# A 20-product first pass and one interleaved table for both passes in a conv and feed-forward kernel

## The chip, the cores and the metric

The kernel runs on one core of a Trainium2 chip. The metric is the time of one execution on the device in microseconds (us); lower is better. The engines are named as in the profile: PE (TensorE, with PEld for its weight loads), DVE (VectorE), ACT (ScalarE), POOL (GpSimd) and SP (SyncE, which issues DMAs).

## The reference

A depthwise causal convolution with 7 taps (weights by softmax, one set for each of 8 heads) over x of (8, 4096, 192), then a feed-forward layer with the quick GELU, all in float32:

```python
w = np.exp(weight - max); w = w / (sum(w) + 1e-9)              # (8 heads, 7 taps)
out = np.einsum('hk,bskhg->bshg', w, x_unf)                    # 7 taps back in time, group = 24
x = out.reshape(8 * 4096, 192)
h = x @ w_in                                                   # (32768, 192) @ (192, 2048)
g = h * (1.0 / (1.0 + np.exp(-1.702 * h)))
return g @ w_out                                               # (32768, 2048) @ (2048, 192)
```

## The kernel before

The tokens are cut into 32 stages ("big"), each of 2 blocks of 512 tokens. In each stage there is a first product (conv output times w_in, `hidden`) and a second one (GELU output times w_out, `second`). Both are written as fast matrix multiplication schemes: sums and differences of blocks of the operands are formed, fewer products than in the plain form are made on PE, and the results are joined. Stage 0 (`first_step`, `second_first`) is done in another way, as it also unpacks the weights and forms their sums (`sums_w_in`, `add_forms`).

**First product.** `hidden` is called twice in a stage, for the two halves v of the columns of w_in. Each pass makes the 21 products of `TERMS`: a pair (sum of w_in blocks, sum of conv blocks). `product1` (L633) issues a product as two matmuls on 64 rows each, side by side on PE, into two PSUM banks. ACT copies results out of PSUM (`copy2`, L670), DVE joins them (`sum2`, L674), and ACT applies the GELU (`gelu`, L655 from PSUM and L659 from SBUF) into the big tile `g`. There are four PSUM tiles of two banks: x, y, z and sums. The products, copies, joins and GELUs stand in the program in the order that the body of `hidden` writes out by hand. `fetch` issues the next pass's first product ahead of its pass.

**Second product.** `second` walks the list `PLAN`. "go" issues one step (three matmuls of 32 columns for the main part and one for a side part, L1007), "sum" and "acc" form sums of blocks of `g` ("acc" by an accumulating DMA on POOL, L983; "sum" on DVE, L391 and L393), "seed" and "join" move results, "turn" and "store" transpose and store. `spot(i)` names blocks of `g`, `room` and `osbs` that hold GELU outputs and their sums; a spot is free once the products that read it are done.

**Conv of the stage after next.** It is made tap by tap, 21 taps for the three channels 1, 0 and 2, in this order. `tap` (L521) is one ACT multiply into a home: tap 0 goes to the conv tile, the others to halves of spots (`TAP_SPOTS`). The taps of channels 1 and 0 are then added together by accumulating DMAs on POOL (L541) listed in `LATER`; (b, i, j) under (c, k) means that behind tap k of channel c, tap j of channel b is added into its tap i, and i = 0 is the conv tile. Taps 1 to 6 of channel 2 are added by POOL (L523). A "tap" in `PLAN` or a `taps_at` in `hidden` draws the next one (`next_tap`): 14 in `second`, 7 in the first pass of the next stage's `hidden`. POOL then forms the sums of the conv (`sums_c`, L391 and L393), and DMAs on SP cross their halves over to the other 64 partitions (`cross`, L561), held in three sets in `conv_t`.

All engines run their instructions in program order; the framework sets a wait before an instruction whose operand another engine or a DMA still writes or reads. SP also loads x (L99) and stores the output (L936).

Of the kernel before, what the change touches and what calls it, by code (L numbers as in the profile page):

```python
# [15 lines left out]
def kernel(  # L16
# [29 lines left out]
    nc = tc.nc  # L46
# [81 lines left out]
    k15, k19, k20, k18, k16 = (room[:, i, :].rearrange("p (h n) -> p h n", h=2) for i in range(5))  # L128
# [27 lines left out]
    NB = 13  # L156
    C11, C12, C21, C22, C31, C32, V2, V3, V4, V5, V6, V7, V8, V1 = range(NB + 1)
    conv_t = consts.tile([P, 3, NB, T], F32)
    SUMS_C = [
        (V1, C31, "-", C11),  # L160
        (V2, V1, "-", C32),
        (V3, C12, "+", V2),
        (V4, C22, "+", V2),
        (V5, C21, "-", V4),
        (V6, C11, "-", V5),
        (V7, C22, "-", C21),
        (V8, C32, "-", C22),
    ]

    def place(big, b):  # L170

        if b == V1:
            return V8 if big % 2 else C31
        return C31 if b == V8 and big % 2 else b

    def own(big):
        return conv_t[:, big % 2 * 2, :, :]
# [6 lines left out]
        (18, 0, "+", 3),  # L184
        (0, 0, "+", 2),
        (12, 10, "n", 11),
        (13, 12, "-", 2),
        (16, 3, "+", 5),
        (17, 2, "+", 5),
        (5, 2, "+", 11),  # L190
        (14, 3, "-", 12),
        (15, 4, "+", 13),
        (19, 6, "+", 8),
        (8, 8, "-", 11),
        (11, 9, "+", 11),
        (9, 9, "-", 3),
        (3, 3, "0", 3),
        (20, 19, "+", 10),
        (12, 1, "-", 13),
        (4, 4, "n", 16),  # L200
        (10, 7, "-", 10),
        (11, 11, "-", 19),
        (7, 7, "+", 19),
# [3 lines left out]
        (14, V2), (10, C21), (20, V5), (6, V3), (19, V6), (0, C11), (17, C32), (5, V8), (4, V7), (8, V1), (12, C22),  # L207
        (9, C12), (13, V4), (3, V3), (15, C22), (16, V6), (2, V1), (1, C21), (11, C11), (7, V7), (18, C12),
# [38 lines left out]
    assert PIECE == CW * D and 3 * PIECE <= NB * T and 3 * PIECE <= 2 * NJ * XW and 3 * PIECE <= FORMS * NG * HD  # L247
# [153 lines left out]
    def sums_w_in(i):  # L401
        add_up(lambda j: w_in_s[:, j, :], *SUMS_W[i])
# [66 lines left out]
    def transpose_x(big, c, n=None):  # L469
# [9 lines left out]
    first_taps = [row(0, k) for k in (6, 7, 10, 11, 14, 15)]  # L479
# [4 lines left out]
        0: [conv_t[:, i, b : b + 2, :] for i in (1, 2) for b in (V2, V4, V6)],  # L484
# [12 lines left out]
    def conv(big, c, k, ns=slice(0, 2), times=vec.tensor_scalar_mul):  # L497
# [50 lines left out]
    def sums_c(big, i):  # L548
        add_up(
            lambda j: own(big)[:, place(big, j), :],  # L550
            *SUMS_C[i],
            eng=vec if big == 1 else nc.gpsimd,
        )

    def cross(big, b0, b1):
        for o in range(2):
            out, src = conv_t[halves[1 - o], 1, b0:b1, :], own(big)[halves[o], b0:b1, :]
            if big == 1 and b1 - b0 > 1:
                act.copy(out, src)
            else:  # L560
                nc.sync.dma_start(out=out, in_=src)  # L561

    def copy_over(b):

        for o in range(2):
            act.copy(conv_t[halves[1 - o], 1, b, :], own(0)[halves[o], b, :])

    waiting = {True: [], False: []}  # L570
    given = {True: 0, False: -1}
    pieces = []

    def cross_now(early, big, b0, b1):
        if early or big == 1:
            cross(big, b0, b1)
        else:
            pieces.extend((big, b, min(b + 3, b1)) for b in range(b0, b1, 3))

    def cross_piece():  # L580
        if pieces:
            cross(*pieces.pop(0))

    def cross_when(early, *what):
        if given[early] < what[0] - 1:
            waiting[early].append(what)
        else:
            cross_now(early, *what)

    def give(early, big):  # L590
        given[early] = big
        for what in waiting[early]:
            cross_now(early, *what)
        waiting[early].clear()

    def prepare(big):

        v1 = place(big, V1)
# [5 lines left out]
        cost = 0.34 if big == 1 else 0.0  # L604
# [8 lines left out]
        yield "", cost, lambda: sums_c(big, 0)  # L613
        yield f"first {big}", 0.0, lambda: cross_when(True, big, v1, v1 + 1)
        yield "", 0.0, lambda: cross_when(False, big, 0, C31)
        for i in range(1, len(SUMS_C)):
            yield "", cost, lambda i=i: sums_c(big, i)
        rest = (C31, V8) if big % 2 else (C31 + 1, NB)
        yield f"all {big}", 0.0, lambda: cross_when(False, big, *rest)
# [8 lines left out]
    def product1(slot, a, b, big, v, first=False):  # L628
        pair = conv_t[:, big % 2 : big % 2 + 2, place(big, b), :]
        for h in range(2):  # L630

            src = pair[halves[h], :, :] if h == big % 2 else pair[halves[h], ::-1, :]
# [9 lines left out]
    def terms(big, v, slot, *ts, first=False):  # L642
        for t in ts:
            product1(slot, *TERMS[t], big, v, first)
            first = False
# [3 lines left out]
    def gelu(b, u, v, src):  # L649
# [3 lines left out]
        if isinstance(src, list):  # L653
            for h in range(2):
                act.activation(  # L655
                    dst[:, :, h, :], src[h].rearrange("p (o t) -> p o t", o=2), AF.Gelu_apprx_sigmoid
                )
        else:
            act.activation(  # L659
                dst.rearrange("p o h t -> p h o t"),  # L660
                src.rearrange("p h (o t) -> p h o t", o=2),
                AF.Gelu_apprx_sigmoid,
            )

    def bank(t, h):
        return t[h] if isinstance(t, list) else t[:, h, :]

    def copy2(dst, src):
        for h in range(2):
            act.copy(bank(dst, h), bank(src, h))  # L670

    def sum2(op, dst, a, b):
        for h in range(2):
            op(*(bank(t, h) for t in (dst, a, b)))  # L674
# [6 lines left out]
    def hidden(big, v, x, z, y, sums, work, fetch, last=lambda: None):  # L681

        def pe(slot, *ts, first=False):
            terms(big, v, slot, *ts, first=first)

        def taps_at(n):
            for _ in range(0 if v else n):
                next_tap()  # L690

        def early(i):
            for item in (EARLY_G if big > 1 else EARLY_G_1)[i] if v else ():
                sum_g(*item)


        if v:
            pe(z, 7, first=True)
            give(True, big)
        if v:  # L700
            pe(sums, 12)
            copy2(k15, sums)
            pe(x, 5, 17)
        else:
            pe(x, 5)
            pe(sums, 12)
            copy2(k15, sums)
            pe(x, 17)
            taps_at(1)
        gelu(B11, 0, v, x)  # L710
        if not v:
            pe(z, 7, first=True)
        pe(sums, 0)
        copy2(k16, sums)
        taps_at(2)
        last()
        def turn_next():
            if big + 2 < N_BIG:
                need(f"done {big + 1}")
                turn_x(big + 2)  # L720

        early(0)
        if not v:
            work(2.0 if big > 1 else 1.6, big + 1)
        elif big == 1:
            work(3.2)

        pe(y, 6, 14, first=True)
        sum2(vec.tensor_sub, x, z, k15)
        early(1)  # L730
        if not v or big == 1:
            work(1.6 if big > 1 else 1.2, big + 1)
        pe(sums, 13)
        copy2(k19, sums)
        pe(x, 2)
        copy2(k18, x)
        taps_at(2)
        pe(z, 11)
        pe(sums, 20, 10)
        sum2(vec.tensor_sub, k15, y, k19)  # L740
        gelu(B12, 0, v, sums)
        pe(x, 4)
        copy2(k20, x)
        sum2(vec.tensor_sub, k19, z, k19)
        early(2)
        if not v or big == 1:
            work(1.1, big + 1)
        gelu(B22, 1, v, k19)
        gelu(B22, 0, v, k15)
        taps_at(2)  # L750
        pe(y, 8)
        pe(sums, 1, 9, first=True)
        pe(y, 15)
        if v and big == 1:
            turn_next()
        elif not v:
# [557 lines left out]
```

## Time and profile before

| | |
|---|---|
| median of 3 runs | 2273.91 us (2273.06 to 2274.0) |
| the profiled execution | 2273.34 us, of it 2271.6 us span from the first to the last instruction |
| PE busy | 2263.5 us (100% of the span) |
| DVE, ACT, POOL busy | 1764.2, 1693.3, 984.9 us |
| moved by DMA | 329.87 MB, 145 GB/s in the mean |

In rows of the timeline and the groups, "L633 PE MATMUL slot<-conv_t,w_in_s" is line 633's matmul that writes a tile named slot; x4 is how many follow each other; "[2.43 <-ACT g L655]" is idle time before it and what ended it. The rows of windows give the length, then for PE, PEld, DVE, ACT and POOL the busy time (and instructions), the granted PE clock, the share of the DMA engines and GB/s. Rows of DMA issues give count, size of each and median time from issue to landing.

### The profile page before, as it was taken

To read this page: it belongs to the slowest core of one execution; us is meant where nothing else is said; L and a number is where in the kernel's file an instruction comes from. 1 tells how busy PE (TensorE), PEld (TensorE's weight loads), DVE (VectorE), ACT (ScalarE), POOL (GpSimd) and SP (SyncE) were. 2 spreads that over 40 slices of the span, in tenths; PEclk is the share of its full clock that TensorE was granted. 3 is DMA by queue.
4 is the path that set the end of the run, shared out by engine and by line. 5 is a ranking of instruction groups with operands and counts; after the bars stand their busy time and mean duration, and the time that the engine had idled before them with its cause. 6 is when DMAs were issued, how large, how long until landed. Compare 5 with 4: busy or idle time off the path is not lost.

```text
span 2271.6 us, 61499 instructions
## 1 busy us (share of the span) xinstructions
PE 2263.5 (100%) x25214; PEld 1210.6 (53%) x25214; DVE 1764.2 (78%) x2591; ACT 1693.3 (75%) x3175; POOL 984.9 (43%) x1008
## 2 busy tenths in 40 slices
PE   9999999999999999999999999999999999999999
PEld 4375555555555555555555555555555555555556
DVE  8987777887777877778877778777887777877777
ACT  8777787777877777777778777787777877777754
POOL 1544454344553445534445434454344553444500
PEclk9999999999999999999999999999999999999999
DMA  9987778777787777777777887778777787776643
GB/s 206 154 158 146 152 139 154 151 147 147 145 154 146 143 145 152 144 150 151 145 152 139 152 156 146 151 138 155 152 144 145 151 149 150 146 144 125 115 99 71
DMA packets 294970, 329.87 MB, mean 145 GB/s; under 512 B 120736, under 2 KB 208800, under 8 KB 294688
## 3 DMA queue, kind: packets, MB, share of 16 engines
q0 software_dynamic: 82704, 196.32, 48.9%
q1 hardware_dynamic: 210336, 129.22, 25.8%
q8 instruction: 198, 3.24, 0.6%
q14 instruction: 84, 0.69, 0.1%
q10 hardware_dynamic: 1648, 0.39, 0.1%
HBM read 53.15 MB, written 25.17 MB: 34 GB/s over the span
## 4 chain that ended last, share of the span: by engine, by line
PE 98%; DMA 1%; DVE 0%; ACT 0%; issue 0%; POOL 0%; SPq 0%; DVEq 0%; ACTq 0%; POOLq 0%
PE slot L633 35%; PE slot L1007 33%; PE sums L633 16%; PE sums L1007 12%; PE slot L839 2%; DMA g<-g 0%; DMA xin<-in_x_dram 0%; ACT conv_t L1114 0%; DVE xt L473 0%; DVE conv_t L504 0%; SPq L99 0%; ACT conv_t L357 0%; POOL g L983 0%; ACT conv_t L356 0%; POOL g L541 0%
## 5 line engine op out<-in xcount | busy, mean ns | idle before, releaser
L633 PE MATMUL slot<-conv_t,w_in_s 64*128 64x512 f32 x3740 | 861.2, 591 | 0.3 <-DVE w_in_s L376 0.3
L1007 PE MATMUL slot<-g,w_form 128*32 128x256 f32 x7024 | 711.1, 379 | 0.1
L633 PEld LDWEIGHTS slot<-conv_t,w_in_s 64*128 64x128 f32 x3740 | 375.6, 187 | 425.6 <-issue 358.9
L393 DVE TENSOR_TENSOR g<-g 128x1024 f32<-128x1024 f32 x372 | 451.5, 1242 | 3.2
L1007 PEld LDWEIGHTS slot<-g,w_form 128*32 128x32 f32 x7024 | 375.6, 110 | 118.1 <-DMA g<-g 0.8
L541 POOL DMA_DIRECT2D g<-g x232 | 225.3, 1084 | 476.0 <-DVE room L393 174.8
L633 PE MATMUL sums<-conv_t,w_in_s 64*128 64x512 f32 x1660 | 407.7, 589 | 0.3 <-DVE w_in_s L376 0.3
L659 ACT ACTIVATE g<-room 128x1024 f32<-128x1024 f32 x310 | 326.0, 1078 | 65.9 <-DVE room L674 40.5
L521 ACT ACTIVATE g<-xt,cw 128x512 f32<-128x512 f32 x534 | 367.8, 725 | 3.7
L1007 PE MATMUL sums<-g,w_form 128*32 128x256 f32 x2648 | 368.8, 379 | 0.0
L1032 ACT COPY room<-slot 32x256 f32<-32x256 f32 x434 | 158.5, 365 | 226.0 <-PE slot L1007 223.1
L1007 PE MATMUL slot<-g,w_out_s 128*32 128x256 f32 x4080 | 318.8, 380 | 0.0
L983 POOL DMA_DIRECT2D g<-g x124 | 126.3, 1019 | 375.9 <-PE slot L1007 143.1
L523 POOL TENSOR_TENSOR conv_t<-conv_t,g 128x512 f32<-128x512 f32 x180 | 250.1, 1389 | 49.0 <-ACT g L521 41.8
L633 PEld LDWEIGHTS sums<-conv_t,w_in_s 64*128 64x128 f32 x1660 | 171.6, 187 | 186.4 <-issue 150.0
L670 ACT COPY room<-slot 128x512 f32<-128x512 f32 x434 | 231.6, 602 | 38.8 <-PE slot L633 38.5
L1007 PEld LDWEIGHTS slot<-g,w_out_s 128*32 128x32 f32 x4080 | 164.7, 110 | 129.0 <-ACT g L655 22.7
L655 ACT ACTIVATE g<-slot 128x512 f32<-128x512 f32 x334 | 180.6, 598 | 46.5 <-POOL conv_t L393 19.0
L393 POOL TENSOR_TENSOR conv_t<-conv_t 128x256 f32<-128x256 f32 x180 | 195.5, 1099 | 11.8 <-DMA conv_t<-g 3.1
L1007 PEld LDWEIGHTS sums<-g,w_form 128*32 128x32 f32 x2648 | 177.8, 110 | 37.6
L674 DVE TENSOR_TENSOR room<-slot,room 128x512 f32<-128x512 f32 x248 | 156.2, 681 | 35.5 <-ACT room L670 35.5
L541 POOL DMA_DIRECT2D conv_t<-g x116 | 145.5, 1254 | 86.3 <-DVE room L391 36.7
(207 smaller groups left out, 2793.9 us busy)
## 6 DMA issues: line engine op xcount, KB each, us to landing
g<-g POOLq DMA_DIRECT2D x124, 512.0 KB, 5.9
g<-g POOLq DMA_DIRECT2D x236, 256.0 KB, 4.8
xin<-in_x_dram SPq DMA_DIRECT2D x240, 180.0 KB, 4.2
conv_t<-conv_t SPq DMA_DIRECT2D x180, 192.0 KB, 3.2
conv_t<-g POOLq DMA_DIRECT2D x118, 256.0 KB, 6.5
out_dram<-osbs SPq DMA_DIRECT2D x186, 128.0 KB, 5.2
g<-room POOLq DMA_DIRECT2D x31, 512.0 KB, 5.4
g<-osbs POOLq DMA_DIRECT2D x30, 512.0 KB, 4.7
```

What stands on the lines that cost most here:

```text
L393: eng.tensor_sub(v(dst), v(a), v(b))
L521: act.mul(home, conv_src(big, c, k), cw[:, c, k : k + 1])
L523: nc.gpsimd.tensor_add(dst, dst, home)
L541: nc.gpsimd.dma_start(out=out, in_=src, accum_op=ALU.add)
L633: nc.tensor.matmul(slot[h], w_in_s[halves[h], a, v * P : (v + 1) * P], src, start=first, stop=True, skip_group_check=True,)
L655: act.activation(dst[:, :, h, :], src[h].rearrange("p (o t) -> p o t", o=2), AF.Gelu_apprx_sigmoid)
L659: act.activation(dst.rearrange("p o h t -> p h o t"), src.rearrange("p h (o t) -> p h o t", o=2), AF.Gelu_apprx_sigmoid,)
L670: act.copy(bank(dst, h), bank(src, h))
L674: op(*(bank(t, h) for t in (dst, a, b)))
L983: nc.gpsimd.dma_start(out=spot(dst), in_=spot(a), accum_op=ALU.add)
L1007: nc.tensor.matmul(dst, w, t, start=first, stop=last, skip_group_check=True)
L1032: act.copy(to, d)
```

## The change

- The first pass of a stage uses a scheme of 20 products, the second its 21. Each pass has its own sums of w_in (`SUMS_W`, 25 and 21 operations on 128 columns each, for 20 on 256 columns before).
- Both passes are one list, `HIDDEN`: products ("mm", pass, term, PSUM tile, first), copies on ACT ("a") or DVE ("v"), joins, GELUs and the rest, interleaved. Copies go to nine places `KS` in `room` and in spots 19, 20, 0 and 1. GELUs can negate their input.
- The sums of the conv are held once, with one copy across, in the places that `places_of` gives; four of them (`SUMS_L`) lie in halves of spots 14 and 17 (`SPOT_V`). POOL forms most of them in "piece" items of `PLAN`, and SP crosses them there.
- `TAP_SPOTS` has spot 20 for 17, channel 2's homes are other halves of spots, some of which are homes of other taps too. 17 taps are drawn in `second`, 4 in `hidden`.

```diff
-    KEPT_LATE, TAP_SPOTS = 3, {0: (13, 15, 17), 1: (11, 10, 16), 2: (14, 16, 18), 3: (15, 16, 19)}
+    KEPT_LATE, TAP_SPOTS = 3, {0: (13, 15, 20), 1: (11, 10, 16)}
+    TAP_HALVES = {2: ((11, 2), (18, 0), (18, 2), (13, 0), (18, 0), (18, 2)), 3: ((12, 2), ...)}
...
+    KS = [room[:, 1, :], room[:, 3, :], room[:, 2, :], room[:, 0, :], room[:, 4, :],
+        spot(19)..., spot(20)..., spot(0)..., spot(1)...]
+    SPOT_V = {16: (14, 2), 17: (14, 0), 18: (17, 2), 19: (17, 0)}
+    SUMS_F = [(12, 1, "+", 4), (12, 12, "-", 5)]
+    SUMS_L = [(16, 0, "-", 6), (17, 7, "-", 3), (18, 0, "-", 2), (19, 0, "-", 1)]
...
-    def hidden(big, v, x, z, y, sums, work, fetch, last=lambda: None):
...
+    HIDDEN = [
+        ("mm", 0, 8, 1, 1), ("tap",), ("tap",), ("mm", 0, 0, 2, 1), ("copy", "a", "k0", "p1", 1), ("mm", 0, 2, 3, 1),
+        ("copy", "v", "k5", "p0", 1), ("copy", "a", "k3", "p2", 1), ("mm", 0, 16, 1, 0),
+        ("copy", "a", "k6", "p3", 1), ("mm", 1, 13, 0, 0), ("copy", "v", "k4", "p1", 1), ("mm", 0, 3, 2, 0),
...
+    ]
+    FETCH, NEXT = (1, 0), (3, 1, 2, 0)
+    def hidden(big, tiles, work):
...
+        for item in HIDDEN:
+            do[item[0]](*item[1:])
...
     LATER = {
         (1, 2): [(1, 1, 2)], (1, 4): [(1, 3, 4)], (1, 6): [(1, 5, 6), (1, 0, 1)], (0, 0): [(1, 3, 5)],
         (0, 2): [(0, 1, 2), (1, 0, 3)], (0, 4): [(0, 3, 4)], (0, 6): [(0, 5, 6), (0, 0, 1)],
-        (2, 2): [(0, 3, 5)], (2, 4): [(0, 0, 3)],
+        (2, 2): [(0, 3, 5)], (2, 3): [(0, 0, 3)],
     }
...
+    def list_pieces(big):
...
+        pieces.append(None)
+        for item in SUMS_L:
+            add(sum_of, big, item)
+        for s in LATE:
+            add(cross_spot, s)
...
     PLAN = [        # the end of it; "piece" items draw from list_pieces
...
-        ("main", 8, 8, "p1", 0, 0, 2), ("go", 1), ("join", "k8", "k9", "+", "k5"), ("tap",), ("go", 1),
+        ("main", 8, 8, "p1", 0, 0, 2), ("piece", 1), ("go", 1),
+        ("join", "k8", "k9", "+", "k5"), ("tap",), ("go", 1), ("join", "k8", "k7", "-", "k8"),
+        ("main", 4, 6, "p4", 0), ("piece", 1), ("go", 1), ("turn", 1, 0, 1, "k10"), ("go", 1),
...
+        ("tap",), ("go", 1), ("turn", 0, 0, 0, "k7"), ("go", 1), ("join", "k6", "k6", "+", "p4"), ("tap",),
+        ("go", 1), ("turn", 1, 1, 1, "k2"), ("tap",), ("go", 1), ("turn", 1, 0, 0, "k6"), ("store", 0, 0),
...
```

More of the change, by code (lines that the diff above doesn't have):

```diff
@@ L546, in end_taps, with sum_of, cross @@
             nc.gpsimd.dma_start(out=out, in_=src, accum_op=ALU.add)
[L548 to L555, printed above, removed]
+    def sum_of(big, item, eng=None):
+        add_up(lambda i: pair(big, i)[:, 0, :], *item, eng=eng or nc.gpsimd)
+    def cross(out, src, eng=None):
         for o in range(2):
-            out, src = conv_t[halves[1 - o], 1, b0:b1, :], own(big)[halves[o], b0:b1, :]
-            if big == 1 and b1 - b0 > 1:
-                act.copy(out, src)
-            else:
-                nc.sync.dma_start(out=out, in_=src)
@@ L563, in copy_over @@
-    def copy_over(b):
[L565 to L571, printed above, removed]
-    pieces = []
[L574 to L580, printed above, removed]
-        if pieces:
[L582 to L594, printed above, removed]
+            if eng is None:
+                nc.sync.dma_start(out=out[halves[1 - o]], in_=src[halves[o]])
+            else:
+                eng(out[halves[1 - o]], src[halves[o]])
+    def cross_run(big, b0, b1, eng=None):
+        (o, x), n = places_of(big, b0), b1 - b0
+        cross(conv_t[:, x : x + n, :], conv_t[:, o : o + n, :], eng)
@@ new lines, in cross_spot, with runs @@
+    def cross_spot(s):
+        cross(spot(s)[:, 1:NG:2, :], spot(s)[:, 0:NG:2, :])
+    V_B = (NR, NR + NV_B)
+    V_F = (V_B[1], V_B[1] + NV_F)
+    V_E = (V_F[1], V_F[1] + NV_E)
+    V_S = (V_E[1], V_E[1] + NV_S)
+    FIRST = V_F if NV_F else (FB, FB + 1)
+    LATE = sorted({s for s, k in SPOT_V.values()})
+    def runs(b0, b1, n=3):
+        return [(i, min(i + n, b1)) for i in range(b0, b1, n)]
+    RAW_RUNS = [r for part in ((0, NR),) for r in runs(*part)]
+    def copy_over(b):
+        o, x = places_of(0, b)
+        for h in range(2):
+            act.copy(conv_t[halves[1 - h], x, :], conv_t[halves[h], o, :])
@@ new lines, in make_common_1, with make_late_1, make_rest_1 @@
+    def make_common_1():
+        for item in SUMS_F + SUMS_B_1:
+            sum_of(1, item, vec)
+        for r in RAW_RUNS + [FIRST] + runs(*V_B):
+            cross_run(1, *r, None if r[1] - r[0] == 1 else act.copy)
+    def make_late_1():
+        for item in SUMS_L:
+            sum_of(1, item, vec)
+        for s in LATE:
+            cross_spot(s)
+    def make_rest_1():
+        for item in SUMS_E + SUMS_S:
+            sum_of(1, item, vec)
+        for r in (V_S, V_E):
+            if r[1] > r[0]:
+                cross_run(1, *r)
@@ L628, in product1 @@
     def product1(slot, a, b, big, v, first=False):
-        pair = conv_t[:, big % 2 : big % 2 + 2, place(big, b), :]
+        both = pair(big, b)
         for h in range(2):
-            src = pair[halves[h], :, :] if h == big % 2 else pair[halves[h], ::-1, :]
+            src = both[halves[h], :, :] if h == 0 else both[halves[h], ::-1, :]
             nc.tensor.matmul(
@@ L640, in product1, with term @@
             )
[L642 to L645, printed above, removed]
+    def term(big, v, t, slot, first):
+        product1(slot, *TERMS[v][t], big, v, first)
     ALL = slice(0, TOK)
@@ L679, in plain, with g_rows @@
             product1(slot, NC * (2 * u + m) + k, 2 * k + n, 0, v, k == first)
-    def hidden(big, v, x, z, y, sums, work, fetch, last=lambda: None):
[L685 to L689, printed above, removed]
+    HIDDEN = [
[25 rows of a table added]
+    ]
+    FETCH, NEXT = (1, 0), (3, 1, 2, 0)
+    def g_rows(i):
+        v, n = i // 8, i % 2
+        r = 2 * (v * len(PAIRS) + i // 2 % 4)
+        return g[:, r // NG, n, :, r % NG : r % NG + 2, :]
@@ L690, in taps_at @@
                 next_tap()
+                work(1.6, 2)
         def early(i):
-            for item in (EARLY_G if big > 1 else EARLY_G_1)[i] if v else ():
+            for item in (EARLY_G if big > 1 else EARLY_G_1)[i]:
                 sum_g(*item)
[L697 to L709, printed above, removed]
@@ L749, in hidden @@
[L749 to L756, printed above, removed]
-            work(2.2 if big > 1 else 1.1, big + 1)
-        sum2(vec.tensor_add, k20, k20, sums)
-        sum2(vec.tensor_sub, k16, y, k16)
-        gelu(B11, 1, v, k20)
-        pe(x, 18)
-        gelu(B21, 1, v, x)
-        early(3)
-        fetch()
-        if not v:
-            copy2(y, z)
-        gelu(B21, 0, v, k16)
@@ L769, in hidden, with over, ve @@
-        if not v:
-            work(1.2, big + 1)
-        if not v and big > 1:
-            turn_next()
-        pe(sums, 3, 19)
-        if not v:
-            work(0.7)
-        sum2(vec.tensor_add, k18, k18, sums)
-        return lambda: gelu(B12, 1, v, k18)
+        def over():
+            if more:
+                need(f"done {big + 1}")
+                for item in SUMS_F:
+                    sum_of(big + 1, item)
+                cross_run(big + 1, *FIRST)
+        def ve(i):
+            if more:
+                need(f"done {big + 1}")
+                sum_of(big + 1, SUMS_E[i])
@@ L779, in chunk_cols @@
+        if big == 1:
+            make_rest_1()
+        do = dict(
+            mm=mm, copy=copy, join=join, gelu=gelu, turn=turn, tap=tap, early=early, over=over, ve=ve,
+            fetch=lambda: fetch(big + 1, tiles[NEXT[0]]) if more else None,
+        )
+        for item in HIDDEN:
+            do[item[0]](*item[1:])
     def chunk_cols(c):
@@ L987, with second @@
     SIDE_HALF = (0, 0, 1, 0, 1, 0, 1)
-    def second(big, bx, by, bs, final, last):
+    def second(big, bx, by, bs, last):
         n3 = NC * Q
@@ L1259, in begin, with fetch @@
         ready.extend(prepare_taps(big))
[L1261 to L1264 removed]
+    def fetch(big, slot):
+        v, t = FETCH
+        term(big, v, t, slot, True)
     def fetch_1():
[L1267 removed]
+        fetch(1, slots[2])
     first_step(fetch_1)
[L1270 removed]
+    tiles = [slots[2], sums, slots[1], slots[0]]
     for big in range(1, N_BIG):
         more = big + 1 < N_BIG
[L1273 to L1276 removed]
+        hidden(big, tiles, work)
+        f, x, a, y = (tiles[i] for i in NEXT)
         if more:
[L1278 removed]
+            list_pieces(big + 1)
         need("forms")
@@ L1281 @@
             begin(big + 2)
-        second(big, x, y, sums, lambda: copy2(sums, z) if more else None, not more)
-        x, z = z, x
+        second(big, x, y, a, not more)
+        tiles = [f, a, x, y]
 _INS = ['x', 'weight', 'moe_w_in', 'moe_w_out']
```

311 lines of the change are left out of this document (170 added, 141 removed), and 87 rows, old and new, of tables (HIDDEN, PLAN, SUMS_W).

## The prediction

> **What bounds the kernel now.** I read the page first (its span, its busy times and its chain), then the chain in order of time for the pace of one product, then one stage cut in two windows at the change from first to second product. The rows of PE's timeline and of the windows are times from the span's start.
>
> ```profile
> span 2271.6 us, 61499 instructions
> PE 2263.5 (100%) x25214; PEld 1210.6 (53%) x25214; DVE 1764.2 (78%) x2591; ACT 1693.3 (75%) x3175; POOL 984.9 (43%) x1008
> PE 98%; DMA 1%; DVE 0%; ACT 0%; issue 0%; POOL 0%; SPq 0%; DVEq 0%; ACTq 0%; POOLq 0%
> ...
> 1011.80 5.15 PE slot L633 x24
> ...
> 1005.52:1041.77 36.25, 36.25 (x172) 16.74 (x169) 23.34 (x34) 30.39 (x51) 22.24 (x21) 1.00 0.76 142
> 1041.77:1075.58 33.81, 33.81 (x627) 20.18 (x625) 30.06 (x44) 22.49 (x49) 9.55 (x11) 1.00 0.79 154
> ```
>
> PE is the path: 98% of the chain, and full in both windows. A product of the first stage leaves four records (two 64-row halves side by side, two records each), so 24 records in 5.15 us are six products at 0.858 us. Forty-two of them are 36.05 us, and the first window is 36.25 us. So a stage is 36.25 + 33.81 = 70.06 us with at most 0.2 us in it that is not product pace. Behind PE, in the first window, DVE is busy 23.34 us, ACT 30.39 and POOL 22.24.
>
> **The change, part by part.**
>
> *One product fewer.* The first pass goes from 21 products to 20, in each of the 31 stages that use the scheme: 31 x 0.858 = 26.6 us off PE. That is the whole gain, and it comes only if PE goes on without waiting.
>
> *DVE and ACT in the first half.* By the built order of one stage, the first half has 32 joins and 6 copies of 128x512 on DVE for 22 joins, and one sum of 128x1024 more (it leaves the second half); the transposes stay. ACT has 24 copies for 22, 20 GELUs of 128x512 for 12, 4 of 128x1024 for 9, and 4 taps for 7.
>
> ```profile
> 1025.20 1.22 DVE L393 TENSOR_TENSOR g<-g 128x1024 f32<-128x1024 f32 x1
> 1031.97 2.47 DVE L674 TENSOR_TENSOR room<-slot,room 128x512 f32<-128x512 f32 x4
> L1114 DVE COPY conv_t<-slot x2: 418/422/426, 13.1 to 13.6; 64x256 f32<-64x256 f32 x2
> 1009.12 1.08 ACT L655 ACTIVATE g<-slot 128x512 f32<-128x512 f32 x2
> 1018.03 2.04 ACT L659 ACTIVATE g<-room 128x1024 f32<-128x1024 f32 x2
> 1008.50 0.73 ACT L521 ACTIVATE conv_t<-xt,cw 128x512 f32<-128x512 f32 x1
> ```
>
> Four joins in 2.47 us are 0.62 each. A DVE copy of 512 columns out of PSUM is not in this trace: it costs at least the 0.42 of the copy of 256 columns, at most twice that; I take a join's 0.62, which moves as many columns. Sixteen more such operations are 16 x 0.62 = 9.9 us (8.7 to 11.2 with the copies' ends), and with the sum DVE rises from 23.3 to some 34.4 of the 35.2 us that 41 products take. ACT gains 10 x 0.54 and loses 5 x 1.02 and 3 x 0.73: 1.9 us less, some 28.5. Neither passes PE, so I cost both at nothing; the cover is under 1 us of DVE slack in the half and the 3.7 us that DVE has free in the second (33.81 - 30.06), and without it a stage grows by the surplus (a rival below).
>
> *Two taps at the head of the stage.* This is where I expect the time to go. A tap is an ACT multiply into a spot of g or room; Pool then adds the taps together by accumulating DMAs, in order. In the kernel before, the taps of channel 2 have homes of their own (spots 14, 16, 18). After, spots 14 and 17 hold sums of the conv, and the home of channel 2's tap 4 is the first half of spot 13, which is also the home of channel 0's tap 1. So tap 4 must wait until the last DMA that reads channel 0's tap 1 has landed: the one into conv_t at the end of channel 0's list, "(0,0,1)". The order of ACT after the change is: the first product is issued, tap 3, tap 4, and only then the copies of the PSUM banks, k0 first. PE may run three products (into banks 1, 2 and 3); the fourth starts bank 1 again and needs k0's copy. What is queued behind the waiting tap on ACT is thus every copy that frees a bank, and PE waits for the first.
>
> When does (0,0,1) land? Here is Pool's timeline before, across the end of a second half; the next stage begins at 1005.52:
>
> ```profile
> 994.35 1.40 POOL L541 DMA_DIRECT2D g<-g  x1
> 994.96 1.68 POOL L541 DMA_DIRECT2D conv_t<-g  x1
> 1002.88 1.74 POOL L541 DMA_DIRECT2D g<-g  x2 [6.24 <-PE slot L1007]
> 1006.71 0.86 POOL L541 DMA_DIRECT2D conv_t<-g  x1 [2.10 <-DVE osbs L925]
> 1007.25 2.09 POOL L541 DMA_DIRECT2D g<-g  x2
> 1009.32 0.90 POOL L541 DMA_DIRECT2D conv_t<-g  x1
> ```
>
> And the times from issue to landing of some of them, by the list of DMA issues for those moments alone (994.35; 1002.88; 1006.71; 1009.32; 1021.00, the last one alone in the queue):
>
> ```profile
> g<-g POOLq DMA_DIRECT2D x1, 256.0 KB, 8.0
> ...
> g<-g POOLq DMA_DIRECT2D x1, 256.0 KB, 3.3
> ...
> conv_t<-g POOLq DMA_DIRECT2D x1, 256.0 KB, 5.5
> ...
> conv_t<-g POOLq DMA_DIRECT2D x1, 256.0 KB, 9.6
> ...
> conv_t<-g POOLq DMA_DIRECT2D x1, 256.0 KB, 3.2
> ```
>
> The wait before 1002.88 is put down to PE, but 994.35 + 8.0 = 1002.35 is the landing that Pool's next DMA needs; 1002.88 + 3.3 = 1006.2 releases 1006.71 in the same way. These are the steps of a chain of DMAs, not of engines. The last of the timeline's rows, 1009.32, is (0,0,1), issued 3.8 us into the stage and landed at 1009.32 + 9.6 - 1005.52 = 13.4 us. Before, nothing needs it there.
>
> After, the first thirteen taps and the accumulations around them stand at the same steps of the second product as before (the fourteenth two steps earlier), so 1006.71, 1.19 us into the stage, holds. Behind it Pool has three new sums of 128x256, a DMA, a fourth sum, a DMA, and then (0,0,1).
>
> ```profile
> 1027.09 1.41 POOL L391 TENSOR_TENSOR conv_t<-conv_t 128x256 f32<-128x256 f32 x2
> 1028.58 4.75 POOL L393 TENSOR_TENSOR conv_t<-conv_t 128x256 f32<-128x256 f32 x4
> ```
>
> A sum is 0.71 to 1.19 us, a DMA issue 0.54 (1006.71 to 1007.25): (0,0,1) is issued at 1.19 + 3 x 0.54 + 4 x (0.71 to 1.19) = 5.7 to 7.6 us. It lands between 5.7 + 3.2 = 8.9 (alone in the queue) and 13.4 (the queue as crowded as before). The issues are spread out now, so I take the middle, 11.0 us. Then the tap (0.73) and two copies (1.08 for a pair): PE's fourth product has its second half at about 12.7 us, when it could have started at 3 x 0.858 = 2.6. The gap is 10.1 us, by the ends 8.0 to 12.5.
>
> *The clock behind the gap.* PE has no gap of this length before, but it has an end and a beginning:
>
> ```profile
> 2265.85 0.38 PE L1007 MATMUL sums<-g,w_form 128*32 128x256 f32 x1
> ...
> 2266.30:2271.30 5.00, 0.00 (x0) 0.00 (x0) 1.47 (x4) 0.33 (x1) 0.00 (x0) 1.00 0.60 123
> 2271.45:2271.60 0.15, 0.00 (x0) 0.00 (x0) 0.00 (x0) 0.00 (x0) 0.00 (x0) 0.50 0.00 0
> L455 PEld LDWEIGHTS sums<-osbs x16: 192/333/338, 1.4 to 5.5; 128*128 128x128 f32 x16
> ```
>
> PE's last matmul ends at 2266.2; the clock is 1.00 to 2271.3 and 0.50 from 2271.45, some 5.2 us after it, and at the start weight loads take 333 ns until about 5 us, then 192. So a gap of 10 us should end on the slow clock, with some 3.5 us (1.4 to 5.0) until it is full again: 3.5 x 0.5 = 1.7 us more. If the clock holds, nothing.
>
> *The start.* In stage 1 the sums of the weights become 46 operations of 128 columns for 20 of 256, and the crossings of two late sums stand on SP behind the output stores and an x load.
>
> ```profile
> L393 DVE TENSOR_TENSOR w_in_s<-w_in_s x7: 420/421/426, 87.7 to 93.2; 128x256 f32<-128x256 f32 x7
> xin<-in_x_dram SPq DMA_DIRECT2D x240, 180.0 KB, 4.2
> conv_t<-conv_t SPq DMA_DIRECT2D x122, 64.0 KB, 3.9
> ```
>
> The sums were 20 x 0.42 = 8.4 us; 46 cost between half that each and as much each, 9.7 to 19.3. With the load and the crossing (4.2 + 3.9) behind them, stage 1 loses 5 to 25 us; I take 15, once.
>
> *What else moves.* The crossings of the sums are 18 DMAs on SP in a stage for 12, and most stand in the second half, a whole half ahead of their use; the one that the next stage's prefetched product needs is issued after product 14 for use behind product 37, 23 x 0.858 = 20 us for a transfer of 3.9: nothing. Merging both passes in one table takes no wait away, since PE has none to lose (0.2 us).
>
> **The sum.** The taps are drawn for stages up to 31, so their tails stand in the first halves of stages 2 to 30: 29 times 10.1 + 1.7 = 11.8, that is 342 us. From the profiled execution, 2273.3 us (0.6 under the median of the runs): 2273.3 - 26.6 + 342 + 15 = 2604 us. A stage goes from 70.1 to 81 us.
>
> **Rivals.** *The DMA lands as if alone:* with the issues spread out the queue may be empty, and the tap waits only to 8.9 us: a gap of 8.0 and the slow clock, 2273.3 - 26.6 + 29 x 9.7 + 15 = 2543 us. For it: the 3.2 and 3.3 us of the two rows that had the queue to themselves; against it: the stage's output stores run then, and every row with a neighbour is at 5.5 or more. The Trainium skill, DMA: Bandwidth & Descriptors, section "Anatomy of one DMA — SWDGE (gpsimd) path", has a fixed 2.0 us and the bytes at 436 GB/s, an estimate of 2.6 us for 256 KB whatever stands in the queue, which would put the landing at 8.3 to 10.2 us; this trace's 3.2 to 9.6 are longer. *The gap is there, the clock holds:* 29 x 10.1 = 293, so 2555 us. For it: only the end and the start show a slow clock. *DVE becomes the bound as well:* if its operations that write PSUM run 10% longer than the joins shown, its 34.4 us pass 37, and with the 2.6 us at the head in which it has no input each stage grows by some 3 us more: 2604 + 29 x 3 = 2691. For it: 34 of 35 us leaves little; against it: DVE can catch up in the second half. *Faster:* (0,0,1) lands before ACT comes to tap 4, about 1.2 us into the stage; then no copy is late, and 2273.3 - 26.6 and up to 10 us of the start give 2247 to 2257. It decides at a landing of about 2.3 us (a bank copy is then just in time for the fourth product); it would have to be issued before 0 and land in 2 us. Against it: before the change that DMA is issued at 3.8 us, behind a chain that the second product's end sets. *The taps do not wait:* if tap 4's home were free, the change would do what it says; the built order has the wait on ACT, so this has the same chance as the last and is counted with it.
>
> **How the numbers follow.** Gap and slow clock 0.50, early landing 0.12, gap with full clock 0.15, gap and DVE 0.17, faster 0.05, and 0.01 for anything that cancels out. The likeliest gives 2604. With the gap between 8.0 and 12.5 us, the clock's 1.7 and the start's 5 to 25, that case alone spans 2273 - 27 + 281 + 5 = 2532 to 2273 - 27 + 412 + 25 = 2683; the case with the full clock goes down to 2273 - 27 + 232 + 5 = 2483, the DVE's above 2700. I give 2500 to 2695. A measurement of this kernel can tell about 0.2%, 4.5 us: faster by more than that 0.05, within it 0.01, slower 0.94.
>
> **What would show it.** Right: in the profile after, a PE gap of 8 to 12 us some 2.6 us into each first half, a clock below 1.00 right behind it, ACT's longest wait at the tap's line on a DMA into conv_t, PE's share near 88%, second halves still 33.8 us, the last stage's first half 35 us. Wrong: first halves of 35 us throughout (the DMA lands early), or long ones whose PE waits are spread over the half and put down to DVE joins.

## The result, and the profile after

The changed kernel takes 2702.56 us in the median (2694.66 to 2709.97) against 2273.91 before: a ratio of 1.189, 95% interval 1.185 to 1.192. The forecast was 2604, the range 2500 to 2695. The direction, the place and the mechanism are as forecast, the size is not: 99 us more, 8 past the upper end.

The profiled execution took 2694.66 us. Its page, the span, the busy times and the granted clock in 40 slices:

```profile
span 2692.9 us, 62943 instructions
...
PE 2333.1 (87%) x25090; PEld 1589.6 (59%) x25090; DVE 2077.0 (77%) x3059; ACT 1706.8 (63%) x3334; POOL 1101.6 (41%) x1218
...
PEclk9899989998899998999989899889989899989899
```

PE is no longer full, and the granted clock is 0.93 in the mean of the execution, with dips all through the kernel. One stage (stage 13, counted from 0), cut at its gap and at the change to the second product; the columns are as in the prediction:

```profile
1109.96:1112.50 2.54, 2.54 (x16) 1.07 (x12) 2.35 (x6) 1.12 (x3) 1.60 (x3) 1.00 0.68 117
1112.50:1123.60 11.10, 0.44 (x3) 0.17 (x2) 0.43 (x1) 1.55 (x3) 9.38 (x11) 0.72 0.97 180
1123.60:1128.50 4.90, 4.90 (x14) 4.03 (x16) 1.46 (x3) 3.55 (x8) 2.16 (x2) 0.60 0.79 150
1128.50:1158.84 30.34, 30.34 (x141) 24.92 (x137) 28.40 (x42) 23.21 (x43) 9.47 (x13) 1.00 0.34 72
...
1158.85:1192.66 33.81, 33.81 (x626) 20.18 (x626) 30.98 (x43) 23.94 (x51) 13.15 (x15) 1.00 0.87 176
```

PE works 2.5 us, stands 11, works on a clock of 0.60 in the mean for 5 us, and then runs at full pace; the second half is 33.81 us as before. Who waits for whom is in the timeline of the same stage, here PE, ACT and POOL one after another:

```profile
1110.92 1.88 PE L709 MATMUL slot<-conv_t,w_in_s 64*128 64x512 f32 x8
1123.46 2.51 PE L709 MATMUL sums<-g,w_in_s 64*128 64x512 f32 x4 [10.66 <-ACT room L799]
...
1110.51 0.72 ACT L562 ACTIVATE g<-xt,cw 128x512 f32<-128x512 f32 x1
1122.03 0.72 ACT L562 ACTIVATE g<-xt,cw 128x512 f32<-128x512 f32 x1 [10.80 <-DMA conv_t<-g]
1122.78 1.07 ACT L799 COPY room<-sums 128x512 f32<-128x512 f32 x2
...
1113.50 1.19 POOL L582 DMA_DIRECT2D g<-g  x1
...
1114.78 1.50 POOL L582 DMA_DIRECT2D g<-g  x1
1115.36 1.81 POOL L582 DMA_DIRECT2D conv_t<-g  x1
```

Tap 3 of channel 2 is drawn at 1110.51; tap 4 is drawn only at 1122.03, after a DMA into conv_t; the bank copies k0 (1122.78) and k3 stand behind it, and PE's fourth product behind k0. POOL's last row is "(0,0,1)", issued 5.4 us into the stage. In the sum over the kernel (waits: total, count, longest):

```profile
ACT g L562 <- DMA conv_t<-g: 336.8, 29, 13.7
DVE room L801 <- PE slot L709: 241.2, 31, 15.5
```

29 waits, 11.6 us each, one in each stage from 2 to 30; DVE's longest waits are for PE, which waits for ACT. The three accumulations of the last rows, by the list of DMA issues for those moments (count, size, us from issue to landing):

```profile
g<-g POOLq DMA_DIRECT2D x1, 256.0 KB, 4.4
...
g<-g POOLq DMA_DIRECT2D x1, 256.0 KB, 5.5
...
conv_t<-g POOLq DMA_DIRECT2D x1, 256.0 KB, 6.7
```

1115.36 + 6.7 is 1122.06: (0,0,1) lands as tap 4 starts. Each DMA behind another takes longer.

By the starts of PE's matmuls, in the mean of stages 2 to 30, a first half is 49.97 us: 41 products of 0.858 are 35.18, the gap 11.64 beyond a product's pace, the slow clock 2.36, and 0.8 are small waits, most of them at the end of the half. The prediction had 47.2.

Stage 1 has two gaps of its own, in PE's timeline:

```profile
100.26 2.92 PE L709 MATMUL slot<-conv_t,w_in_s 64*128 64x512 f32 x5 [5.46 <-DVE osbs L1014]
...
118.56 3.87 PE L709 MATMUL slot<-conv_t,w_in_s 64*128 64x512 f32 x8 [11.65 <-DMA conv_t<-conv_t]
```

The first is the 46 sums of w_in on DVE ahead of the output's transposes, the second the crossing on SP behind the output stores and the x load, both of which the prediction names; it had 15 us for them, the trace has 23.

### The profile page after: what moved, and what is told of

The parts are those of the page before. It is cut to its first block, busy times and chain, and to the rows that moved or that the text cites. A ratio compares the mean times of both kernels' runs of the same rounds, so it can differ in the third digit from the quotient of the medians.

```text
span 2692.9 us, 62943 instructions
## 1 busy us (share of the span) xinstructions
PE 2333.1 (87%) x25090; PEld 1589.6 (59%) x25090; DVE 2077.0 (77%) x3059; ACT 1706.8 (63%) x3334; POOL 1101.6 (41%) x1218
## 5 line engine op out<-in xcount | busy, mean ns | idle before, releaser
L709 PE MATMUL slot<-conv_t,w_in_s 64*128 64x512 f32 x3372 | 910.8, 611 | 17.9 <-DMA conv_t<-conv_t 11.6
L709 PEld LDWEIGHTS slot<-conv_t,w_in_s 64*128 64x128 f32 x3372 | 605.4, 196 | 193.2 <-issue 69.1
L432 POOL TENSOR_TENSOR conv_t<-conv_t 128x256 f32<-128x256 f32 x300 | 289.0, 1034 | 479.8 <-PE slot L709 200.6
L1097 PE MATMUL sums<-g,w_form 128*32 128x256 f32 x3800 | 422.4, 379 | 0.4 <-DMA g<-g 0.3
L818 ACT ACTIVATE g<-slot 128x512 f32<-128x512 f32 x494 | 265.5, 625 | 129.4 <-PE slot L709 74.7
L709 PE MATMUL slot<-g,w_in_s 64*128 64x512 f32 x556 | 192.4, 648 | 176.2 <-ACT room L799 176.2
L709 PEld LDWEIGHTS sums<-conv_t,w_in_s 64*128 64x128 f32 x1284 | 224.8, 193 | 66.1 <-issue 18.8
L1097 PEld LDWEIGHTS sums<-g,w_form 128*32 128x32 f32 x3800 | 210.4, 110 | 70.9 <-DMA g<-g 1.3
L709 PEld LDWEIGHTS slot<-g,w_in_s 64*128 64x128 f32 x556 | 105.7, 201 | 204.4 <-POOL conv_t L564 188.2
L801 DVE COPY room<-slot 128x512 f32<-128x512 f32 x62 | 40.0, 686 | 241.2 <-PE slot L709 241.2
```

The costliest lines, as they stand in the source:

```text
L432: eng.tensor_sub(v(dst), v(a), v(b))
L709: nc.tensor.matmul(slot[h], w_in_s[halves[h], a, v * P : (v + 1) * P], src, start=first, stop=True, skip_group_check=True,)
L801: vec.tensor_copy(out, i)
L818: act.activation(dst[:, :, h, :], ot(bank(src, h)), AF.Gelu_apprx_sigmoid, scale=float(sign))
L1097: nc.tensor.matmul(dst, w, t, start=first, stop=last, skip_group_check=True)
```

## The experiments

Two theories were compared. One wait: the shared home of tap 4 is the whole loss. Waits in layers: behind it stand others that it hides. For the sizes: is it the queue that makes (0,0,1) late, and does the slow clock cost what the trace shows?

**tap4_own_home.**

```diff
-    TAP_HALVES = {2: ((11, 2), (18, 0), (18, 2), (13, 0), (18, 0), (18, 2)), ...}
+    TAP_HALVES = {2: ((11, 2), (18, 0), (18, 2), (11, 0), (18, 0), (18, 2)), ...}
```

> Only the home of channel 2's tap 4 changes: from the first half of spot 13 (channel 0's tap 1) to the first half of spot 11, which nothing reads at that time. Theory 1, one wait: the ACT wait at that tap is the whole loss of a stage (14.8 us in each of 29 first halves); without it only what little is left of the other operands counts, first halves of 35 to 37 us, some 2270 to 2330 us. Theory 2, waits in layers: ACT now comes to the copy k6 into spot 20, the home of channel 0's taps 5 and 6, and that copy waits for the DMA that reads tap 5 (landed 15.9 to 16.4 us into the stage in the changed kernel); and PE's fourth product reads a late sum whose crossing, the DMA g<-g on SP, is issued at 3.3 to 4.1 us and landed by some 6 to 8. So PE stands twice, 4 to 5 us in front of the fourth product and 5 to 8 in front of the seventh: first halves of 45 to 50 us, 2560 to 2710 us.

2720.37 us, ratio 1.196 (1.195 to 1.198): no gain at all, and 10 us past the upper end of the layers' forecast. PE and ACT in stage 13 (it starts at 1119.47), and ACT's wait over the kernel:

```profile
1126.37 2.24 PE L709 MATMUL sums<-g,w_in_s 64*128 64x512 f32 x4 [4.06 <-DMA g<-g]
1136.25 2.56 PE L709 MATMUL slot<-conv_t,w_in_s 64*128 64x512 f32 x4 [4.37 <-ACT g L799]
...
1135.61 1.07 ACT L799 COPY g<-slot 128x512 f32<-128x512 f32 x2 [12.17 <-DMA g<-g]
...
ACT g L799 <- DMA g<-g: 374.7, 29, 15.9
```

ACT's wait at the tap is gone and stands at the copy into g, k6, instead: spot 20 is also the home of channel 0's taps 5 and 6. PE stands in front of the fourth product for the late sum's crossing (DMA g<-g), and again in front of the seventh. First halves are 50.88 us for 49.97. One wait as the only cause is refuted. That the time even rises is the clock's doing: by the starts and the clock records the two waits of a half are 10.1 us together for the 11.6 of the one, but the clock falls twice in each of the 29 halves, and 9.2 us of work at 0.50 cost 4.6 us, for 2.3 in the changed kernel.

**own_homes.**

```diff
-    TAP_HALVES = {2: ((11, 2), (18, 0), (18, 2), (13, 0), (18, 0), (18, 2)), ...}
+    TAP_HALVES = {0: ((13, 0), (13, 2), (15, 0), (15, 2), (11, 2), (10, 2)),     # takes the place of TAP_SPOTS[0]
+                  2: ((9, 2), (18, 0), (18, 2), (11, 0), (16, 2), (16, 0)), ...}
```

> All of channel 0's and channel 2's taps get homes that neither a copy of the first half nor another channel's tap waits for (channel 0: spots 13, 15, second halves of 11 and 10; channel 2: halves of 9, 18, 11 and 16). Theory 1 (the shared homes are the only cause): no gap, first halves of 35.2 to 36 us, 2270 to 2295 us. Theory 2 (layers): the crossing of the late sums in spot 14 is next, since PE's fourth product reads it: a gap from 2.3 us to some 6.5 or 8, put down to a DMA g<-g issued by SP, 4 to 5.5 us, with little or no slow clock behind it; first halves of 39 to 41.5 us and 2385 to 2460 us.

2585.59 us, ratio 1.136 (1.133 to 1.140): 117 us less than the changed kernel, 126 more than the upper end of the layers' forecast. PE and DVE in stage 13:

```profile
1077.82 2.17 PE L709 MATMUL sums<-g,w_in_s 64*128 64x512 f32 x4 [4.22 <-DMA g<-g]
1090.83 1.29 PE L709 MATMUL slot<-conv_t,w_in_s 64*128 64x512 f32 x3 [1.68 <-DVE sums L812]
...
1088.88 1.29 DVE L812 TENSOR_TENSOR osbs<-sums,room 128x512 f32<-128x512 f32 x2 [3.28 <-DMA out_dram<-osbs]
```

The gap at the crossing is there as expected. Two things were not: the slow clock behind it costs 3.1 us a stage (6.1 us at 0.50 in the mean), and there is a third layer: DVE's join k8 goes to osbs, which the output stores still read. First halves are 46.20 us. The clock records tell why a gap of 4.9 us costs more slow clock than one of 12: of the 12.2 us at 0.50 in a half of the changed kernel, 7.6 pass inside the gap, while PE stands anyway; here the gap ends sooner, only 1.4 of 7.5 us pass inside it, and in 12 of the 29 halves the clock falls a second time, behind the wait for k8.

**homes_and_order**, with the homes of own_homes.

```diff
-        ("main", 8, 8, "p1", 0, 0, 2), ("piece", 1), ("go", 1),      # and three more ("piece", 1) behind it
+        ("main", 8, 8, "p1", 0, 0, 2), ("piece", 4), ("go", 1),
-        (0, 0): [(1, 3, 5)], (0, 2): [(0, 1, 2), (1, 0, 3)], (0, 4): [(0, 3, 4)], ...
+        (0, 3): [(1, 3, 5), (0, 1, 2)], (0, 4): [(1, 0, 3), (0, 3, 4)], ...
-                cross_run(1, *r)
+                cross_run(1, *r, act.copy)                            # in make_rest_1
```

> Own homes as in the run before, and besides: Pool forms the four late sums in one go, ahead of the DMAs of taps that it waits for (the accumulation of channel 1's tap 5 into 3 and those behind it are issued behind them); and stage 1's last crossings are ACT copies for SP DMAs. If the layers end there, first halves are 35.2 to 36 us, stage 1's second gap (12.8 us, and the slow clock behind it) shrinks to 2 or 3, and the kernel takes what the product saved less what the start costs: 2273 - 27 + 5 to 10, with up to 0.5 us a stage of small waits: 2250 to 2270 us. Rival: DVE with some 34.4 us of work in 35.2 becomes the bound once nothing else holds PE: first halves of 36.5 to 38 us, PE waits spread over the half and put down to joins, 2295 to 2340 us.

2537.93 us, ratio 1.117 (1.115 to 1.120); 198 us past the upper end of the rival's forecast and 268 past that of the first. The gap at the fourth product is gone, and stage 1's first half is 55.1 us, for 61.1 in the changed kernel. The gap now stands further on, at the join k8 (stage 13, then DVE's waits over the kernel):

```profile
1061.64 2.67 PE L709 MATMUL slot<-conv_t,w_in_s 64*128 64x512 f32 x4 [4.95 <-DVE sums L812]
...
1059.69 1.29 DVE L812 TENSOR_TENSOR osbs<-sums,room 128x512 f32<-128x512 f32 x2 [5.89 <-DMA out_dram<-osbs]
...
DVE osbs L812 <- DMA out_dram<-osbs: 155.6, 28, 7.3
```

The layers were not at their end: the wait for the output stores grew from 3.28 to 5.89 us in this stage, since everything ahead of it now comes earlier and the stores don't.

**all_places.**

```diff
-        spot(1)...                                                   # the place of k8
+        spot(18)..., spot(14)...                                     # k8, and k9 for k7's first use
-    TAP_HALVES = {2: ..., 3: ...}
+    TAP_HALVES = {1: ((11, 0), (11, 2), (16, 0), (10, 0), (10, 2), (16, 2)), 0: ((15, 0), (15, 2), (13, 0), (13, 2), (8, 2), (12, 2)), 2: ((8, 0), (11, 2), (7, 0), (7, 2), (16, 2), (16, 0)), ...}
-        ("mm", 0, 8, 1, 1), ("tap",), ("tap",), ...                  # the second one behind the copy k6
-        (2, 2): [(0, 3, 5)], (2, 3): [(0, 0, 3)],
+        (2, 4): [(0, 3, 5)], (2, 6): [(0, 0, 3)],
```

> Built on the order and the stage-1 copies of homes_and_order, with every place of the first half free when it is written: the join k8 and the first copy k7 go to spots 18 and 14 instead of osbs, which the output stores read until some 16 us into the stage; the taps of all three channels get halves of spots that nothing early overwrites (channel 1: 11, 16, 10; channel 0: 15, 13, 8, 12; channel 2: 8, 11, 7, 16); one of the two taps at the head stands four copies later, and the last accumulations behind the taps. If the loss was a stack of waits, of which the prediction saw only the first, no gap over 1 us is left: first halves of 35.2 to 36 us, and with the start (18 us more than before in homes_and_order's trace, 8 of them made good by the copies already) 2273 - 27 + 10 to 18, up to 0.5 us a stage: 2252 to 2280 us, granted clock 0.99 to 1.00. Rival, DVE as the bound: its 34.4 us do not fit beside the waits of joins for products, first halves of 36.5 to 38.5 us with PE waits put down to DVE spread over the half, 2295 to 2355 us.

2303.9 us, ratio 1.013 (1.012 to 1.015). Its page:

```profile
PE 2271.3 (99%) x25090; PEld 1281.0 (56%) x25090; DVE 2099.9 (91%) x3059; ACT 1697.2 (74%) x3338; POOL 1121.3 (49%) x1218
```

399 us of the 429 between the two kernels go with these edits: the free places, the order of Pool's sums and of the taps, the slow clock behind the waits, which is gone from stages 2 to 30, and 8.7 us in stage 1 (61.1 to 52.4). The edits were not run one by one from here, so the parts are not shown apart. In stages 2 to 30 no two starts of PE lie over 1.6 us apart. First halves are 36.60 us, past the forecast; this and the time lie in the rival's range. Yet PE's waits in those stages are not put down to DVE but to ACT (17 are long enough to be listed, 7.5 us in all): by the starts, 0.47 us a stage stand at the copy k9 on ACT and 0.5 where the second product begins.

**start_and_head.**

```diff
-        ("copy", "a", "k6", "p3", 1), ("tap",), ... ("mm", 0, 18, 0, 0), ("tap",), ...
+        ("copy", "a", "k6", "p3", 1), ("tap",), ... ("copy", "a", "k9", "p0", 1), ("tap",), ...
         store(0, 1)
+        make_rest_1()
+        sums_w_in(1 - FETCH[0])                                      # was ahead of the turns
```

> all_places with two more edits. One tap of the head stands behind the copy k9 instead of ahead of it, since the tenth product lost 0.47 us a stage to that copy (0.94 us a stage in all by the starts of the matmuls). And in the start the late sums and crossings of stage 1, and the turns of stage 0's output, stand on DVE and ACT ahead of the first pass's 25 sums of w_in, and two taps of stage 2 leave spot 18 for spot 11. In all_places a stage's first half was 36.60 us for 41 products of 0.858 (35.2): 0.94 us of waits at products, 0.5 at its end, where the second product waits for the last GELUs. If those are what is left, first halves go to 35.7 to 36.1, stage 1 gains 2 to 5 us, and the time is 2270 to 2290 us: the scheme with one product fewer then saves 0.1 to 0.5 us a stage against the kernel before (36.25), which the start (12 to 14 us) takes back. Rival: DVE, with its 34.4 us, holds some other product instead; first halves stay at 36.3 to 36.8 us and the time at 2290 to 2305.

2282.25 us, ratio 1.0040 (1.0027 to 1.0054): the time is inside the forecast, and still 0.4% slower than the kernel before. One stage, and the gaps of PE that are left in stage 1:

```profile
665.78:701.69 35.91, 35.91 (x168) 22.96 (x164) 32.72 (x50) 29.14 (x55) 19.91 (x22) 1.00 0.77 150
701.70:735.50 33.80, 33.80 (x625) 20.09 (x624) 31.67 (x43) 23.74 (x51) 15.72 (x19) 1.00 0.87 178
...
96.72 2.08 PE L710 MATMUL sums<-conv_t,w_in_s 64*128 64x512 f32 x4 [3.69 <-DVE w_in_s L431]
...
114.04 1.29 PE L710 MATMUL slot<-conv_t,w_in_s 64*128 64x512 f32 x3 [1.76 <-DVE sums L813]
```

First halves are 36.17 us in the mean (36.25 before): of the 0.858 us that the missing product saves, 0.08 are left. The 0.47 us at k9 are gone with a tap moved on ACT, and DVE has as much to do as in all_places, so DVE was not the bound there; it is busy 32.72 of 35.91 us. By the starts, 0.4 of the 0.858 goes where the second product begins (0.94 us behind the last product's start, 0.53 before) and the rest in small waits spread over the half. That place is a wait for ACT: the second product starts 0.05 us behind the end of the GELU it needs in the mean of the 29 stages, for 0.72 before; no run moved that GELU. The start, up to the end of stage 1, is 9 us longer than before (174.1 for 164.7) and takes more than the halves give.

**warm_products.**

```diff
+            if (v, t, to) == (0, 2, 3) and 1 < big < N_BIG - 1:
+                for _ in range(12):
+                    term(big, v, t, tiles[to], True)
             term(big, v, t, tiles[to], bool(first))
```

> Changed kernel, with twelve extra products (12 x 0.858 = 10.3 us of PE work whose result is overwritten) in front of its third product, in stages 2 to 30: they fill the gap of 11.2 to 14.1 us while ACT waits. If the half clock behind the gap costs what the trace of the changed kernel shows (4.6 us at half clock, 2.3 us a stage), the time falls by 29 x 2.3 = 67 us to some 2635 us, and the granted clock stays at 1.00. If the slow clock is only beside the path (ACT and DVE being the bound there), the time stays within 15 us of 2702.

2656.75 us, ratio 1.169 (1.167 to 1.170): 46 us less than the changed kernel with 29 x 12 products more, 22 short of the forecast. By the starts, the extra products and the wait behind them take 10.30 + 1.33 us, the gap as it was; the products behind it lose 0.9 us a stage to small waits, where the slow clock took 2.36. So the clock term is real, and two thirds of the forecast 67 us come back; the small waits take the other third. Stage 24, cut at the wait that is left, one of three behind which the clock still falls:

```profile
2000.64:2013.20 12.56, 12.56 (x64) 5.72 (x60) 2.78 (x6) 1.12 (x3) 9.62 (x12) 1.00 0.90 163
2013.20:2016.30 3.10, 1.33 (x7) 0.59 (x5) 0.00 (x0) 2.15 (x4) 1.38 (x2) 1.00 1.01 181
2016.40:2019.70 3.30, 3.30 (x10) 1.66 (x8) 1.38 (x2) 1.86 (x5) 0.91 (x2) 0.50 0.59 125
```

**no_stores and head_of_queue.**

```diff
-            if stored[n] == 2:
+            if stored[n] == 2 and (big == 1 or big == N_BIG - 2):    # no_stores: the output of stages 2 to 29 isn't stored
```

```diff
-        (0, 4): [(0, 3, 4)], (0, 6): [(0, 5, 6), (0, 0, 1)],
+        (0, 4): [(0, 0, 1), (0, 3, 4)], (0, 6): [(0, 5, 6)],         # head_of_queue
```

> Changed kernel without the output stores of stages 2 to 29 (28 x 6 DMAs on SP left out). In the changed kernel (0,0,1) was issued at 5.9 us and landed at 12.8, not 11.0. If the output stores, which start at 7 us, slow it, it lands now by 10 to 11 us and a stage is 1.5 to 3 us shorter: 2610 to 2660 us. If the accumulations ahead of it in Pool's own queue set it (three DMAs issued at 3.7, 5.0 and 5.6 us landed at 8.3, 10.6 and 12.5), it lands at 12 to 12.8 still, and the time is 2680 to 2705 us.

> Changed kernel with (0,0,1) issued first of the three (behind channel 0's tap 4 in place of its tap 6), the accumulations of tap 4 into 3 and 6 into 5 behind it. If the queue sets the landing, it takes the first place: landed at 7.5 to 9 us, and ACT's wait at tap 4 ends 4 to 5 us earlier. If the DMA itself takes some 7 us at that time whatever stands ahead of it, it lands at 10.5 to 11. By the layers the time hardly follows: the copy k6 then waits for the accumulation of tap 5 into 3, which lands at 16 us or later, so that the gap only moves behind the sixth product: 2640 to 2720 us; with tap 4's wait as the only cause it would be 2560 to 2590 us.

no_stores, which leaves the output of 28 stages unstored: 2695.69 us, ratio 1.185 (1.183 to 1.188), as the changed kernel; (0,0,1) took 6.9 us in its stage 13 and landed at 12.86 us in the mean of 29 stages (12.84 with the stores). head_of_queue: 2737.27 us, ratio 1.204 (1.201 to 1.206), 17 past the forecast's upper end. (0,0,1), by the list of DMA issues of each kernel for that moment, no_stores first:

```profile
conv_t<-g POOLq DMA_DIRECT2D x1, 256.0 KB, 6.9
```

```profile
conv_t<-g POOLq DMA_DIRECT2D x1, 256.0 KB, 4.3
...
ACT g L562 <- DMA conv_t<-g: 210.6, 29, 9.1
ACT g L799 <- DMA g<-g: 184.9, 29, 7.2
```

The place in Pool's queue sets the landing: 8.44, 10.89 and 12.84 us for the three in the changed kernel, 8.47, 10.02 and 12.57 when (0,0,1) is the first. ACT's wait at tap 4 shrinks by 126 us in all, and 185 us of waiting appear at k6: a wait shortened in the first layer is handed to the second. PE's two waits are 10.7 us a half together for 11.6, but as in tap4_own_home the clock falls twice, and the slow clock costs 4.5 us for 2.3.

## Why the prediction was wrong in size

*One product fewer, -26.6.* Right as PE's work, not as time: in the best version 0.08 us a stage remain of 0.858. DVE's load was forecast well enough (34.4 us; 32.64 in the sum of the windows above, 32.72 in start_and_head), but only the 0.2 us of before was counted for the ends of the half.

*The wait at tap 4.* Right in place, order and releaser, and the issue of (0,0,1) at 5.7 to 7.6 us was 5.87. The step that failed, the term that was mis-sized most, is its landing: 11.0 us taken, as the middle between a DMA alone (8.9) and a crowded queue (13.4; the middle itself is 11.15); it was 12.84, because the issues are not spread out: three follow within 2 us, and each lands some 2 us behind the one ahead of it. The trace of before could have told: there the four accumulations up to (0,0,1) land at 6.47, 8.63, 10.91 and 12.92 us in the mean of the same stages, 2.0 to 2.3 us apart, and (0,0,1) is issued at 3.31. Issued 2.6 us later after the change, it landed at the same time. The gap beyond a product's pace is 11.64 us for 10.1: 29 x 1.54 = 45 us.

*The slow clock.* 2.36 us a stage for 1.7: 19 us. *The ends of the half:* 0.8 us for the 0.2 of before: 17 us. *Stage 1:* 23 for 15: 8 us. Together 89 us, and 2604 + 89 = 2693 for the profiled 2694.66. The gap, the slow clock and stage 1 each came out inside the bounds that the prediction gave them, but all above the value that it took, and the ends of the half had no bounds. The median of the four runs is 8 us above the profiled one; what those 8 us are is not shown.

*The rivals.* The early landing (2543) fell by the queue, the full clock (2555) by the clock behind the gap and by warm_products. DVE as the bound came out near the measured time (2691) for another reason: the row of DVE's waits shows it waiting for PE. The rival "faster" held that tap 4 is all that stands between 2604 and 2250; tap4_own_home shows that to be wrong. The crossing of the late sums was costed at nothing in "what else moves": that counts the one that the prefetched product needs and not the one that the fourth product reads, which was issued 3.3 us into the stage. It cost nothing only as long as ACT's wait covered it. The places of k6 (spot 20) and of k7 and k8 (osbs) were missed in the same way.

What stays open: how much of the 2 us between two landings is due to the transfers beside them. The output stores are not it (no_stores), but the four crossings of the late sums on SP, issued from 3.3 us on, run at the same time in both, and no run leaves them out.

## What to carry to other kernels

When a change gives buffers a second user, list for every early writer of the next stage the last reader of its place (a queued DMA, a crossing, an output store), and when that one lands; the first wait found hides the others, and removing it alone gave nothing here. Two short waits can cost more than one long one, if the clock falls behind each. A DMA's landing is read from the issue of the first one in its run of the queue, not from its own. A saved product is worth its time only where the engines around it can close up as well.

## What the runs showed of the hardware

- Accumulating DMAs of 256 KB, issued close together in one queue, land one after another, 1.6 to 2.6 us apart in the two orders; leaving out the output stores beside them changed nothing (12.84 and 12.86 us).
- The granted clock falls to 0.50 within the gap (in the 29 stages of the changed kernel, by its clock records, 2.8 to 5.5 us behind the last start of a matmul) and stays there for 10.24 or 13.65 us; in warm_products for 3.41. These are multiples of 3.41 us. The Trainium skill, TensorE: Matmul & The Clock Gate, section "Part 1: The HAM clock gate", has a free-running window of 3413 ns, and by that the trace agrees.
- It took less than such a window without work: in warm_products distances of 3.27, 2.68 and 2.37 us between two starts (0.43 at full pace; the shortest is in stage 24, shown above) were each followed by 3.41 us at 0.50, while 2.16 and below left the clock at 1.00. The same section of the Trainium skill speaks of an idle window of some 3.4 us; here the shorter gaps sufficed.
- The length of a gap alone does not decide it: in own_homes a distance of 1.97 us (at 1329.23) was followed by 0.50 and one of 2.84 (at 2211.24) was not. All changes of the clock in a trace lie on one grid of 3.41 us. Cut along that grid, seven traces have 248 falls between 180 us and the last 40 us: each came at the end of a window in which PE was busy at most 0.61 of the time, and every window behind which the clock stayed at 1.00 has at least 0.42 (the ends of matmuls are modelled, so the shares are rough). So the share of work in a window fits what is seen, with the limit near one half; no run was made to find it.
